# First loads in halves over two queues, a warm-up on constants, unpinned transfers, and a scan whose rounding moves

## The chip, the cores and the metric

The kernel runs on one core of a Trainium2 chip. The metric is the device time of one execution in microseconds (us); the median of three runs of the kernel before is 1250.3 us (1250.12 to 1250.6).

## The reference, cut to what matters

Two independent parts are computed and laid side by side in the last dimension of the output (2048 rows, 1024 + 1024 columns, bf16).

Part A is a diagonal state-space layer: `Bu = x · B_bar^T` with a complex `B_bar`, a scan `h = Lam_bar * h + Bu[t]` over 2048 steps, and `y = 2 Re(h · C^T) + x * D`. Part B is attention over segments of 32 rows with 8 memory rows each, 32 heads of 128:

```python
for s in range(n_seg):
    h = concat([mem, x[:, s*32:(s+1)*32]])       # 8 + 32 rows
    q, k, v = h·Wq, h·Wk, h·Wv
    p = softmax(where(mask, q·k^T * scale, -1e9))
    o = (p·v)·Wo
    mem = o[:, :8];  outs.append(o[:, 8:])
```

## The kernel before, in words

The kernel has four phases; the change touches the first (the pool `p1`, up to about 350 us). That phase computes all values `v = x · Wv` of part B and the first product and scan of part A, woven together. `b.xe` holds part B's x with its 1024 inner elements on the partitions (eight groups of 128) and rows along the free dimension.

**Values.** `Wv` is cut into eight blocks `hb` of 512 columns. For each, sixteen tiles of 128 rows are computed by eight matmuls each (`v_mm`, 128x512, L411) into one of four PSUM banks: `k.ps("A")` alternates between the tags P and S, each with two buffers. ScalarE (ACT) evicts a tile to SBUF (`k.copy("s", ...)`, recorded at L75), and one DMA stores two tiles to a scratch tensor `b_vx` in DRAM (`v_st`, L419). Two tiles make a pair. `v_tile` gives each of the first eight pairs a staging buffer of its own (`st0`), and all later pairs one of two buffers `b_vst`. The generator `values()` takes pairs of blocks 0 and 1 first, then blocks 2 to 7 in order.

**Start.** The first four row tiles of x come as plain rows (`load_rows`, four DMAs of 256 KB) on the queues of SP (SyncE) and ACT, with the weights of block 0 in four quarters. TensorE (PE) turns each by eight transposes with an identity (`turn_rows`), which are then evicted into `b.xe`. Before that, six matmuls on a zeroed tile warm PE up. The rest of x is loaded by transposing DMAs (`load_x` of part B, L367).

**Part A, stage 1.** 32 steps n = 4 pc + tb. Each takes 16 matmuls (L256) of a block of B (`load_b`, two transposing DMAs, L237) with a block of transposed x (`xT[tb]`, `load_x` of part A, one transposing DMA of 1 MB, L231) into one of two `psO` buffers of two banks. VectorE (DVE) multiplies it by cosine and sine tables (L263, L264), subtracts (L266), adds (L267), and runs two scans (L270, L271). The result is rounded to bf16 by ACT and multiplied back by DVE (`post`: L288 to L292). Between steps PE computes three or four value tiles, so that values and scan finish together.

**Order.** The instructions of each engine are placed by a scheduler that follows dependencies and its own estimates. `tc.keep_in_program_order(...)` pins an instruction to its place in the program; an unpinned DMA may be moved past other DMAs of its queue. A DMA signals landing by one of eight semaphores, taken in turn over both queues, so each DMA also waits for the landing of the one eight before it. In the kernel before, the xT loads of part A are pinned, and so are, up to step 3, the value weights of blocks 2 and later and the stores `v_st`.

Of the kernel before, what the change touches and what calls it, by code (L numbers as in the profile page):

```python
# [9 lines left out]
BF16 = mybir.dt.bfloat16  # L10
I32 = mybir.dt.int32
ACT = mybir.ActivationFunctionType
ALU = mybir.AluOpType
# [120 lines left out]
class PartA:  # L134
# [92 lines left out]
    def load_x(self, tb):  # L227
        k = self.k
        self.xT[tb] = k.w8((KC, TB), "xT")
        k.tc.keep_in_program_order(  # L230
            k.SP.dma_start(self.xT[tb], self.x[0][tb * TB:(tb + 1) * TB, :], transpose=True))  # L231

    def load_b(self, pc):
        k = self.k
# [12 lines left out]
    def stage1(self, pc, tb):  # L247
        k = self.k; V, PE = k.V, k.PE
        pin = k.tc.keep_in_program_order
        if tb == 0:  # L250
            self.carry = None
        cs, rot, ed = self.tabs
        u = k.ps("O")
        for i in range(2):
            for c in range(KC):
                m = PE.matmul(u[:, i, :], self.bt[:, i, c, :], self.xT[tb][:, c, :], start=(c == 0), stop=(c == KC - 1))  # L256
                if self.pin:
                    pin(m)
        c_ = cs[:, 0, 0:TB].unsqueeze(1).to_broadcast([128, 2, TB])
        s_ = cs[:, 1, 0:TB].unsqueeze(1).to_broadcast([128, 2, TB])  # L260
        a = self.wp.tile([128, 2, TB], FP32, name="a_a")
        b = self.wp.tile([128, 2, TB], FP32, name="a_b", bufs=1)
        V.tensor_tensor(a[:], u[:], c_, ALU.mult)  # L263
        V.tensor_tensor(b[:], u[:], s_, ALU.mult)  # L264
        wr, wi = a[:, 0, :], a[:, 1, :]
        V.tensor_tensor(wi, wi, b[:, 0, :], ALU.subtract)  # L266
        V.tensor_tensor(wr, wr, b[:, 1, :], ALU.add)  # L267
        rb = self.rr[:, pc:pc + 1].to_broadcast([128, TB])
        ini = self.carry
        pin(V.tensor_tensor_scan(wr, rb, wr, 0.0 if ini is None else ini[:, 0:1], ALU.mult, ALU.add))  # L270
        pin(V.tensor_tensor_scan(wi, rb, wi, 0.0 if ini is None else ini[:, 1:2], ALU.mult, ALU.add))  # L271
        if tb < NB - 1:
            nx = self.wp.tile([128, 2], FP32, name="a_nx"); tt = self.wp.tile([128, 2], FP32, name="a_tt")
            V.tensor_scalar(tt[:], ed[:, 0:2], wi[:, TB - 1:TB], None, ALU.mult)
            V.scalar_tensor_tensor(nx[:], ed[:, 2:4], wr[:, TB - 1:TB], tt[:], ALU.mult, ALU.add)
            self.carry = nx
        if tb not in self.hs:
            self.hs[tb] = self.hsp.tile([128, PC, 2, TB], BF16, name="a_hs", bufs=4)
        self.prev, self.last = self.last, [a, rot, self.hs[tb][:, pc, :, :]]

    def post(self, last):
        if last is None:
            return
        k = self.k; V = k.V
        pin = k.tc.keep_in_program_order
        a, rot, hp = last
        g = self.wp.tile([128, 2, TB], BF16, name="a_g", bufs=1)
        pin(k.S.activation(g[:], a[:], ACT.Copy))  # L288
        n = self.wp.tile([128, 2, TB], BF16, name="a_n", bufs=1)
        pin(V.tensor_tensor(hp, g[:, 0:1, :].to_broadcast([128, 2, TB]), rot[:, 0:2, :], ALU.mult))  # L290
        pin(V.tensor_tensor(n[:], g[:, 1:2, :].to_broadcast([128, 2, TB]), rot[:, 1:3, :], ALU.mult))
        pin(V.tensor_tensor(hp, hp, n[:], ALU.add))  # L292

    def stage2(self, pool, dB):

# [21 lines left out]
class PartB:  # L317
# [48 lines left out]
            if lo < hi:  # L366
                k.SP.dma_start(self.xe[:, :, lo:hi], self.x[0][lo + r:hi + r, :], transpose=True)  # L367

    def load_rows(self, t, n, xr, e):
        e.dma_start(xr[:, t:t + n, :], self.x[0][t * 128 + 64:(t + n) * 128 + 64, :].rearrange("(i p) d -> p i d", p=128))  # L370

    def turn_rows(self, t, xr):

        k = self.k
        pt = k.ps("O", (128, 1024), BF16)
        for c in range(KC):
            k.tc.keep_in_program_order(k.PE.transpose(pt[:, c * 128:(c + 1) * 128], xr[:, t, c * 128:(c + 1) * 128], k.ident[:]))
        k.copy("vs"[t % 2], self.xe[:, :, t * 128:(t + 1) * 128], pt[:].rearrange("p (c n) -> p c n", c=KC))

    def sum_x(self, q, pool):  # L380

# [16 lines left out]
    def load_wv(self, hb, w=None, parts=1, e=None, js=None):  # L398
        if w is None:
            w = self.k.w8((KC, 512), "wv")  # L400
        n = KC // parts
        for i in js or range(parts):
            d = (e or self.k.SP).dma_start(w[:, i * n:(i + 1) * n, :], self.Wf[2][:, i * n:(i + 1) * n, hb * 512:(hb + 1) * 512])
            if self.pin and hb > 1:
                self.k.tc.keep_in_program_order(d)
        return w


# [6 lines left out]
    def v_st(self, hb, q, st, e):  # L415
        vx = self.vx[hb]
        s0 = GX + 2 * q * 128
        n = 2 if q < 7 else 1
        d = e.dma_start(vx[s0:s0 + n * 128, :].rearrange("(i p) n -> p i n", p=128), st[:, 0:n, :])  # L419
        if self.pin:  # L420
            self.k.tc.keep_in_program_order(d)
        if q == 7:
            e.dma_start(vx[0:64, :], st[0:64, 1, :])
            e.dma_start(vx[T - 32:T + 32, :], st[64:128, 1, :])
# [16 lines left out]
    def v_first(self, w, xr, e):  # L441

        k = self.k
        for t in range(3):
            self.turn_rows(t, xr)
        p = [k.ps("A") for t in range(4)]
        for j in range(4):
            for t in range(3):
                self.v_mm(p[t], t, w, range(2 * j, 2 * j + 2))
            if j == 2:  # L450
                self.turn_rows(3, xr)
        self.v_mm(p[3], 3, w, range(KC))
# [393 lines left out]
def kernel_main(tc, A_x, A_Lre, A_Lim, A_Bre, A_Bim, A_Cre, A_Cim, A_logdt, A_Dskip, B_x, B_mem0, B_Wq, B_Wk, B_Wv, B_Wo, out,  # L846
                force=False, dbg=None):
    with ExitStack() as ctx:
        k = K(tc, ctx)
        k.dbg = dbg  # L850
        nc = k.nc
        consts(k)
        a = PartA(k, A_x, A_Lre, A_Lim, A_Bre, A_Bim, A_Cre, A_Cim, A_logdt, A_Dskip, out)
# [11 lines left out]
        with pool("p1", "right") as p1:  # L865
# [6 lines left out]
            a.tab = a.wp = a.btp = b.vst = p1  # L872
            a.jf = b.rall[:, 0:TB + 1]
            xr = tmp[:, 4096:8192].rearrange("p (t d) -> p t d", t=4)
            b.load_rows(0, 1, xr, k.SP)
            b.load_rows(1, 1, xr, nc.scalar)
            b.load_rows(2, 1, xr, k.SP)
            for j in range(4):
                b.load_wv(0, wvs[0], 4, (nc.scalar, k.SP)[j % 2], [j])
            b.load_rows(3, 1, xr, nc.scalar)  # L880
            b.load_wv(1, wvs[1], 2)
            a.load_params(tmp)
            k.SP.dma_start(tmp[0:M, 0:D], b.mem0[0])
            b.load_x(512, 1024)
            b.load_x(1024, 1536)
            b.load_x(1536, T)
            wu = tmp[:, 2048:2560]
            k.V.memset(wu, 0.0)
            pw = k.ps("O")
            for i in range(6):  # L890
                k.PE.matmul(pw[:, i % 2, :], wu[:, 0:128], wu, start=True, stop=True)

            def values():
                yield from b.v_first(wvs[0], xr, k.SP)
# [7 lines left out]
            v = values()  # L902
            done = 0
# [16 lines left out]
            for n in range(PC * NB):  # L920
                pc, tb = n // NB, n % NB
                a.stage1(pc, tb)
                if n in (0, 1):
                    a.load_x(2 + n)
                    wvs[2 + n] = b.load_wv(2 + n)
                if tb == 1 and pc + 1 < PC:
                    nbt = a.load_b(pc + 1)
                want = 20 + 4 * (n + 1) if n < 4 else 36 + (92 * (n - 3) + 27) // 28
                half = done + 2
                while done < want:  # L930
                    next(v, None); done += 1
                    if done == half:
                        a.post(a.prev)
                while done >= 32 and oged < done // 16:
                    b.og(oged, wvs.pop(oged))
                    oged += 1
                if pc + 1 < PC:
                    if tb == 0:
                        tabs = a.tables(pc + 1)
                    else:  # L940
                        next(tabs)
                    if tb == 3:
                        a.tabs, a.bt = a.ntabs, nbt
# [12 lines left out]
            k.V.memset(b.rall[:], 0.0)  # L956
            a.load_c(1, 0)
            a.load_c(1, 1)
# [151 lines left out]
```

## Time and profile before

| What | us |
|---|---|
| median of three runs | 1250.3 |
| profiled execution | 1250.12 |
| its span from first to last instruction | 1248.4 |
| PE busy in the span | 1236.3 |
| DVE busy | 609.4 |
| ACT busy | 329.3 |
| POOL (GpSimd) busy | 199.5 |

The times of the page are from one profiled execution, and start at its first instruction. "SPq" and "ACTq" rows are DMAs as the queue's engine issues them: their time is that of the issue, not of the transfer. In a row of the timeline the first number is the start, the second the duration; a bracket at its end gives the idle time before it and what ended that. In a table of groups, after the bar: busy time, mean ns of one, idle time before them.

### The profile page before, as it was taken

To read this page: it belongs to the slowest core of one execution; us is meant where nothing else is said; L and a number is where in the kernel's file an instruction comes from. 1 tells how busy PE (TensorE), PEld (TensorE's weight loads), DVE (VectorE), ACT (ScalarE), POOL (GpSimd) and SP (SyncE) were. 2 spreads that over 40 slices of the span, in tenths; PEclk is the share of its full clock that TensorE was granted. 3 is DMA by queue.
4 is the path that set the end of the run, shared out by engine and by line. 5 is a ranking of instruction groups with operands and counts; after the bars stand their busy time and mean duration, and the time that the engine had idled before them with its cause. 6 is when DMAs were issued, how large, how long until landed. Compare 5 with 4: busy or idle time off the path is not lost. (4 is left out here: it accounts for less than half of the span.)

```text
span 1248.4 us, 19205 instructions
## 1 busy us (share of the span) xinstructions
PE 1236.3 (99%) x7852; PEld 651.9 (52%) x7923; DVE 609.4 (49%) x1117; ACT 329.3 (26%) x757; POOL 199.5 (16%) x284
## 2 busy tenths in 40 slices
PE   9999999999999999999999999999999999999998
PEld 4444444444455445555555655555556554454443
DVE  4889999999931122444444444444444450011000
ACT  4444434444210002323333333333233320000000
POOL 2000000000032130222222222322232230000000
PEclk9999999999999999999999999999999999999999
DMA  9932232333666557576767544645575469606000
GB/s 238 261 109 68 89 98 71 91 93 85 151 213 201 138 163 139 96 141 141 142 122 156 114 122 94 129 82 94 105 139 105 72 195 217 159 18 152 17 26 19
DMA packets 296995, 151.81 MB, mean 122 GB/s; under 512 B 138440, under 2 KB 290240, under 8 KB 296904
## 3 DMA queue, kind: packets, MB, share of 16 engines
q1 hardware_dynamic: 295640, 149.11, 51.9%
q8 instruction: 63, 1.03, 0.4%
q10 hardware_dynamic: 1264, 1.44, 0.4%
q14 instruction: 28, 0.23, 0.1%
HBM read 73.70 MB, written 43.66 MB: 94 GB/s over the span
## 5 line engine op out<-in xcount | busy, mean ns | idle before, releaser
L570 PE MATMUL psP<-b_xe,w 128*128 128x480 bf16 x2048 | 439.7, 366 | 0.0
L570 PEld LDWEIGHTS <-w 128*128 128x128 bf16 x2048 | 194.2, 98 | 185.2
L603 POOL TENSOR_TENSOR b_m<-b_e,maskB 99x396 bf16<-99x396 bf16 x160 | 139.2, 871 | 356.3 <-ACT b_e L599 356.3
L77 DVE CAST b_q<-psP 128x480 bf16<-128x480 f32 (+1 forms) x192 | 98.2, 533 | 150.9 <-PE psP L570 139.4
L411 PEld LDWEIGHTS <-b_xe 128*128 128x128 bf16 x1024 | 99.9, 98 | 120.4 <-ACT b_xe L75 0.6
L670 PEld LDWEIGHTS <-b_ol 128*128 128x128 bf16 x1024 | 99.5, 98 | 117.5
L75 ACT ACTIVATE b_k<-psP 128x480 bf16<-128x480 f32 x128 | 73.1, 571 | 314.3 <-PE psP L570 314.3
L599 ACT ACTIVATE b_e<-psS 99x396 bf16<-99x396 f32 x176 | 87.4, 496 | 173.8 <-PE psS L596 166.6
L621 DVE TENSOR_TENSOR b_ot<-psO,b_rall 99x512 bf16<-99x512 f32 x176 | 121.7, 692 | 6.4
L256 PE MATMUL psO<-w,a_bt 128*128 128x512 bf16 x496 | 114.8, 379 | 0.8
L670 PE MATMUL psS<-w,b_ol 128*128 128x512 bf16 x438 | 99.0, 379 | 0.6
L619 DVE RECIPROCAL b_rall<-psO 99x4 f32<-99x4 f32 x176 | 31.2, 177 | 136.3 <-PE psO L614 136.2
L411 PE MATMUL psS<-w,b_xe 128*128 128x512 bf16 x378 | 90.1, 379 | 0.4
L411 PE MATMUL psP<-w,b_xe 128*128 128x512 bf16 x376 | 89.8, 379 | 0.4
L256 PEld LDWEIGHTS <-a_bt 128*128 128x128 bf16 x512 | 49.7, 98 | 59.0
L310 PEld LDWEIGHTS <-a_hs 128*128 128x128 bf16 x512 | 49.5, 98 | 58.3
L614 PE MATMUL psO<-b_v,b_m 99*128 99x129 bf16 x704 | 70.5, 221 | 0.1
L77 DVE CAST b_ost<-psS 128x512 bf16<-128x512 f32 x13 | 9.0, 692 | 125.4 <-PE psS L670 112.3
L596 PEld LDWEIGHTS <-b_k 128*128 128x128 bf16 x704 | 49.8, 98 | 33.4 <-issue 0.5
L596 PE MATMUL psS<-b_q,b_k 128*128 128x99 bf16 x704 | 60.1, 208 | 0.2
L75 ACT ACTIVATE b_vst<-psS 128x512 bf16<-128x512 f32 x56 | 33.4, 597 | 98.1 <-PE psS L411 70.2
L310 PE MATMUL psS<-w,a_hs 128*128 128x512 bf16 x245 | 57.3, 380 | 0.6
(201 smaller groups left out, 1084.0 us busy)
## 6 DMA issues: line engine op xcount, KB each, us to landing
b_v<-b_vx SPq DMA_DIRECT2D x16, 1056.0 KB
b_os<-b_ot SPq DMA_DIRECT2D x16, 960.0 KB
w<-in_B_Wv_dram SPq DMA_DIRECT2D x14, 1024.0 KB
b_vx<-b_vst SPq DMA_DIRECT2D x48, 256.0 KB
w<-in_B_Wo_dram SPq DMA_DIRECT2D x12, 1024.0 KB
w<-in_B_Wq_dram SPq DMA_DIRECT2D x16, 512.0 KB
w<-in_B_Wk_dram SPq DMA_DIRECT2D x16, 512.0 KB
a_xn<-in_A_x_dram SPq DMA_DIRECT2D x32, 128.0 KB
```

Of the source, the lines that this page charges most:

```text
L75: self.S.activation(out, in_, ACT.Copy)
L77: self.V.tensor_copy(out, in_)
L256: m = PE.matmul(u[:, i, :], self.bt[:, i, c, :], self.xT[tb][:, c, :], start=(c == 0), stop=(c == KC - 1))
L310: PE.matmul(py[:], self.hs[tb][:, pc, i, tt * 128:(tt + 1) * 128], self.ct[half, i][:, pc, :], start=(pc == 0 and i == 0), stop=(pc == PC ...
L411: m = self.k.PE.matmul(p[:], self.xe[:, c, t * 128:(t + 1) * 128], w[:, c, :], start=(c == 0), stop=(c == KC - 1))
L570: PE.matmul(p[:, 0:480], w[:, i * KC + c, hh * 128:(hh + 1) * 128], self.xe[:, c, 480 * q:480 * q + 480], start=(c == 0), stop=(c == KC - 1))
L596: PE.matmul(s[:, j * GW:(j + 1) * GW], kt[:, hh, g0:g0 + 128], qt[:, hh, g0:g0 + GW], start=True, stop=True)
L599: k.S.activation(e[:], s[0:GW, 0:4 * GW], ACT.Exp, scale=float(E) ** -0.5, accum_out=self.accE[0:GW, i:i + 1])
L603: k.G.tensor_tensor(v4(m[:, 0:4 * GW]), v4(e[:]), mask[0:GW, :, :].unsqueeze(2).to_broadcast([GW, 2, 2, GW]), ALU.mult)
L614: PE.matmul(o[:, gg, cs], m[:, j * GW:j * GW + 128], vt[:, 2 * u + gg, cs], start=True, stop=True)
L621: V.tensor_tensor(ot[:, 2 * u:2 * u + 2, :].rearrange("p g (h e) -> p g h e", h=2), oa[:, :, 1:257].rearrange("p g (h e) -> p g h e", h=2) ...
L670: k.PE.matmul(self.acc[t, half], ol[:, h8, tt * 128:(tt + 1) * 128], self.wo_half(half, h), start=(h == 0), stop=(h == H - 1))
```

## The change

- **Loads at the start.** Each of the four row tiles of x is loaded as two halves of 512 columns, one on SP's queue and one on ACT's, and after each row tile two eighths of block 0's weights follow, one on each queue.
- **Warm-up.** Eight matmuls instead of six, on a constant tile of ones that exists already, instead of a tile that DVE zeroes.
- **Turned tiles.** Value matmuls are placed between the turns as their inputs come; each turn is evicted by two copies on DVE instead of one on DVE or ACT.
- **Pins.** The xT loads of part A, the value weights and the stores of values are no longer pinned.
- **Stage 1.** The subtraction L266 moves to POOL. The rounding on ACT (`round`) is placed behind the next step's matmuls, the multiplication back (`post`) behind the next step's scans, only the first of its three instructions pinned, where before all four were pinned two value tiles into the step after.

```diff
     def load_x(self, tb):
-        k.tc.keep_in_program_order(
-            k.SP.dma_start(self.xT[tb], self.x[0][tb * TB:(tb + 1) * TB, :], transpose=True))
+        k.SP.dma_start(self.xT[tb], self.x[0][tb * TB:(tb + 1) * TB, :], transpose=True)
...
+        self.round()
...
-        V.tensor_tensor(wi, wi, b[:, 0, :], ALU.subtract)
+        k.G.tensor_tensor(wi, wi, b[:, 0, :], ALU.subtract)
...
+        self.post()
         if tb not in self.hs:
             self.hs[tb] = self.hsp.tile([128, PC, 2, TB], BF16, name="a_hs", bufs=4)
-        self.prev, self.last = self.last, [a, rot, self.hs[tb][:, pc, :, :]]
-
-    def post(self, last):
...
-        g = self.wp.tile([128, 2, TB], BF16, name="a_g", bufs=1)
-        pin(k.S.activation(g[:], a[:], ACT.Copy))
-        n = self.wp.tile([128, 2, TB], BF16, name="a_n", bufs=1)
-        pin(V.tensor_tensor(hp, g[:, 0:1, :].to_broadcast([128, 2, TB]), rot[:, 0:2, :], ALU.mult))
-        pin(V.tensor_tensor(n[:], g[:, 1:2, :].to_broadcast([128, 2, TB]), rot[:, 1:3, :], ALU.mult))
-        pin(V.tensor_tensor(hp, hp, n[:], ALU.add))
+        self.last = [a, rot, self.hs[tb][:, pc, :, :]]
+
+    def round(self):
+        if self.last is not None:
+            k = self.k
+            g = self.wp.tile([128, 2, TB], BF16, name="a_g", bufs=1)
+            k.tc.keep_in_program_order(k.S.activation(g[:], self.last[0][:], ACT.Copy))
+            self.last[0] = g
+
+    def post(self):
+        if self.last is None:
+            return
+        V = self.k.V
+        g, rot, hp = self.last
+        self.last = None
+        n = self.wp.tile([128, 2, TB], BF16, name="a_n", bufs=1)
+        self.k.tc.keep_in_program_order(
+            V.tensor_tensor(hp, g[:, 0:1, :].to_broadcast([128, 2, TB]), rot[:, 0:2, :], ALU.mult))
+        V.tensor_tensor(n[:], g[:, 1:2, :].to_broadcast([128, 2, TB]), rot[:, 1:3, :], ALU.mult)
+        V.tensor_tensor(hp, hp, n[:], ALU.add)
...
-    def load_rows(self, t, n, xr, e):
-        e.dma_start(xr[:, t:t + n, :], self.x[0][t * 128 + 64:(t + n) * 128 + 64, :].rearrange("(i p) d -> p i d", p=128))
+    def load_rows(self, t, xr):
+        for i, e in enumerate((k.SP, k.S)):
+            cs = slice(i * 512, (i + 1) * 512)
+            k.tc.keep_in_program_order(e.dma_start(xr[:, t, cs], self.x[0][t * 128 + 64:t * 128 + 192, cs]))
     def turn_rows(self, t, xr):
-        pt = k.ps("O", (128, 1024), BF16)
+        pt = k.ps("O", (128, 2, 1024), BF16)
...
-        k.copy("vs"[t % 2], self.xe[:, :, t * 128:(t + 1) * 128], pt[:].rearrange("p (c n) -> p c n", c=KC))
+        for i in range(2):
+            k.copy("v", self.xe[:, 4 * i:4 * i + 4, t * 128:(t + 1) * 128], pt[:, i, 0:512].rearrange("p (c n) -> p c n", c=4))
...
-            if self.pin and hb > 1:
-                self.k.tc.keep_in_program_order(d)
...
-        if self.pin:
-            self.k.tc.keep_in_program_order(d)
...
     def v_first(self, w, xr, e):
-        for t in range(3):
+        p = [k.ps("A") for t in range(4)]
+        for t, todo in enumerate(((), ((0, 0, 4), (1, 0, 4)), ((0, 4, 6), (1, 4, 6), (2, 0, 6)),
+                                  ((0, 6, 8), (1, 6, 8), (2, 6, 8), (3, 0, 8)))):
             self.turn_rows(t, xr)
-        p = [k.ps("A") for t in range(4)]
-        for j in range(4):
-            for t in range(3):
-                self.v_mm(p[t], t, w, range(2 * j, 2 * j + 2))
-            if j == 2:
-                self.turn_rows(3, xr)
-        self.v_mm(p[3], 3, w, range(KC))
+            for tt, c0, c1 in todo:
+                self.v_mm(p[tt], tt, w, range(c0, c1))
...
-            b.load_rows(0, 1, xr, k.SP)
-            b.load_rows(1, 1, xr, nc.scalar)
-            b.load_rows(2, 1, xr, k.SP)
-            for j in range(4):
-                b.load_wv(0, wvs[0], 4, (nc.scalar, k.SP)[j % 2], [j])
-            b.load_rows(3, 1, xr, nc.scalar)
+            for t in range(4):
+                b.load_rows(t, xr)
+                for j in range(2):
+                    b.load_wv(0, wvs[0], KC, (k.SP, nc.scalar)[j], [2 * t + j])
...
-            wu = tmp[:, 2048:2560]
-            k.V.memset(wu, 0.0)
+            one = nc.const_aps.tensor(1.0, [128, 512], BF16)
...
-            for i in range(6):
-                k.PE.matmul(pw[:, i % 2, :], wu[:, 0:128], wu, start=True, stop=True)
+            for i in range(8):
+                k.PE.matmul(pw[:, i % 2, :], one[:, 0:128], one, start=True, stop=True)
...
-                half = done + 2
                 while done < want:
                     next(v, None); done += 1
-                    if done == half:
-                        a.post(a.prev)
...
-            a.post(a.last)
+            a.round()
+            a.post()
```

More of the change, by code (lines that the diff above doesn't have):

```diff
@@ L276, in stage1 @@
             self.carry = nx
+        self.post()
         if tb not in self.hs:
             self.hs[tb] = self.hsp.tile([128, PC, 2, TB], BF16, name="a_hs", bufs=4)
-        self.prev, self.last = self.last, [a, rot, self.hs[tb][:, pc, :, :]]
-    def post(self, last):
-        if last is None:
-            return
-        k = self.k; V = k.V
-        pin = k.tc.keep_in_program_order
-        a, rot, hp = last
-        g = self.wp.tile([128, 2, TB], BF16, name="a_g", bufs=1)
-        pin(k.S.activation(g[:], a[:], ACT.Copy))
+        self.last = [a, rot, self.hs[tb][:, pc, :, :]]
[7 more added lines that the diff above has]
+        if self.last is None:
+            return
+        V = self.k.V
+        g, rot, hp = self.last
+        self.last = None
         n = self.wp.tile([128, 2, TB], BF16, name="a_n", bufs=1)
-        pin(V.tensor_tensor(hp, g[:, 0:1, :].to_broadcast([128, 2, TB]), rot[:, 0:2, :], ALU.mult))
-        pin(V.tensor_tensor(n[:], g[:, 1:2, :].to_broadcast([128, 2, TB]), rot[:, 1:3, :], ALU.mult))
-        pin(V.tensor_tensor(hp, hp, n[:], ALU.add))
+        self.k.tc.keep_in_program_order(
+            V.tensor_tensor(hp, g[:, 0:1, :].to_broadcast([128, 2, TB]), rot[:, 0:2, :], ALU.mult))
+        V.tensor_tensor(n[:], g[:, 1:2, :].to_broadcast([128, 2, TB]), rot[:, 1:3, :], ALU.mult)
+        V.tensor_tensor(hp, hp, n[:], ALU.add)
     def stage2(self, pool, dB):
@@ L367, in load_x @@
                 k.SP.dma_start(self.xe[:, :, lo:hi], self.x[0][lo + r:hi + r, :], transpose=True)
-    def load_rows(self, t, n, xr, e):
-        e.dma_start(xr[:, t:t + n, :], self.x[0][t * 128 + 64:(t + n) * 128 + 64, :].rearrange("(i p) d -> p i d", p=128))
+    def load_rows(self, t, xr):
+        k = self.k
+        for i, e in enumerate((k.SP, k.S)):
+            cs = slice(i * 512, (i + 1) * 512)
+            k.tc.keep_in_program_order(e.dma_start(xr[:, t, cs], self.x[0][t * 128 + 64:t * 128 + 192, cs]))
     def turn_rows(self, t, xr):
         k = self.k
-        pt = k.ps("O", (128, 1024), BF16)
+        pt = k.ps("O", (128, 2, 1024), BF16)
         for c in range(KC):
-            k.tc.keep_in_program_order(k.PE.transpose(pt[:, c * 128:(c + 1) * 128], xr[:, t, c * 128:(c + 1) * 128], k.ident[:]))
-        k.copy("vs"[t % 2], self.xe[:, :, t * 128:(t + 1) * 128], pt[:].rearrange("p (c n) -> p c n", c=KC))
+            k.tc.keep_in_program_order(k.PE.transpose(pt[:, c // 4, (c % 4) * 128:(c % 4) * 128 + 128], xr[:, t, c * 128:(c + 1) * 128], k.ident[:]))
+        for i in range(2):
+            k.copy("v", self.xe[:, 4 * i:4 * i + 4, t * 128:(t + 1) * 128], pt[:, i, 0:512].rearrange("p (c n) -> p c n", c=4))
     def sum_x(self, q, pool):
@@ L402, in load_wv @@
         for i in js or range(parts):
-            d = (e or self.k.SP).dma_start(w[:, i * n:(i + 1) * n, :], self.Wf[2][:, i * n:(i + 1) * n, hb * 512:(hb + 1) * 512])
-            if self.pin and hb > 1:
-                self.k.tc.keep_in_program_order(d)
+            (e or self.k.SP).dma_start(w[:, i * n:(i + 1) * n, :], self.Wf[2][:, i * n:(i + 1) * n, hb * 512:(hb + 1) * 512])
         return w
@@ L418, in v_st @@
         n = 2 if q < 7 else 1
-        d = e.dma_start(vx[s0:s0 + n * 128, :].rearrange("(i p) n -> p i n", p=128), st[:, 0:n, :])
-        if self.pin:
-            self.k.tc.keep_in_program_order(d)
+        e.dma_start(vx[s0:s0 + n * 128, :].rearrange("(i p) n -> p i n", p=128), st[:, 0:n, :])
         if q == 7:
```

## The prediction

> **What bounds the kernel now.** I read the page's engine shares and clock row first.
>
> ```profile
> PE 1236.3 (99%) x7852; PEld 651.9 (52%) x7923; DVE 609.4 (49%) x1117; ACT 329.3 (26%) x757; POOL 199.5 (16%) x284
> PEclk9999999999999999999999999999999999999999
> ```
>
> TensorE is busy for 1236.3 of 1248.4 us at full clock, so only work or waits on PE can move the end. The table of PE's waits (total, times, longest) is short:
>
> ```profile
> PE psO L891 <- DVE a_hs L888: 1.3, 1, 1.3
> PE psO L377 <- DMA a_hs<-in_B_x_dram: 0.5, 1, 0.5
> PE psO L377 <- DVE b_xe L77: 0.3, 1, 0.3
> ```
>
> All three lie in the first 6.4 us. So the change can gain at most some 2 us at the start, and it can lose wherever it makes PE wait. I therefore looked for the thinnest cover: SyncE's (SP) queue from 25 to 70 us in order of time (start, issue time, engine, line, transfer),
>
> ```profile
> 29.26 4.42 SPq L231 DMA_TRANSPOSE w<-in_A_x_dram  x1
> ...
> 40.27 0.67 SPq L419 DMA_DIRECT2D b_vx<-b_vst  x1
> 40.99 5.59 SPq L231 DMA_TRANSPOSE w<-in_A_x_dram  x1
> 46.67 0.53 SPq L419 DMA_DIRECT2D b_vx<-b_vst  x1
> 47.26 4.78 SPq L231 DMA_TRANSPOSE w<-in_A_x_dram  x1
> 52.09 0.57 SPq L403 DMA_DIRECT2D w<-in_B_Wv_dram  x1
> 52.76 1.07 SPq L419 DMA_DIRECT2D b_vx<-b_vst  x2
> 53.88 7.89 SPq L231 DMA_TRANSPOSE w<-in_A_x_dram  x1
> 61.82 0.57 SPq L403 DMA_DIRECT2D w<-in_B_Wv_dram  x1
> 62.50 7.09 SPq L419 DMA_DIRECT2D b_vx<-b_vst  x3
> ```
>
> then who waits for it on ACT (in brackets: idle time before, and what ended it), and PE beside it,
>
> ```profile
> 59.87 0.60 ACT L75 ACTIVATE b_vst<-psS 128x512 bf16<-128x512 f32 x1 [6.42 <-DMA b_vx<-b_vst]
> ...
> 68.63 0.60 ACT L75 ACTIVATE b_vst<-psS 128x512 bf16<-128x512 f32 x1 [4.82 <-DMA b_vx<-b_vst]
> ```
>
> ```profile
> 56.10 1.89 PE L411 MATMUL psS<-a_hs,b_xe 128*128 128x512 bf16 x8
> ...
> 59.55 1.89 PE L411 MATMUL psS<-a_hs,b_xe 128*128 128x512 bf16 x8
> ```
>
> and the table of stretches (the last columns are granted clock, DMA share, GB/s).
>
> ```profile
> 55.00:60.00 5.00, 5.00 (x25) 2.27 (x24) 3.65 (x4) 0.13 (x1) 0.00 (x0) 1.00 1.10 311
> ```
>
> I number the pairs of value tiles in the order in which they are computed, from 0. Pairs 0 to 7 go to eight buffers of their own; from pair 8 on there are two buffers `b_vst`, so pair 10 may be evicted only when the store of pair 8 has landed, pair 11 after that of pair 9. In the queue above, the stores of pairs 8, 9, 10 and 11, 12 are issued at 40.27, 46.67, 52.76, 62.50. ACT already waits: pair 12's eviction starts at 59.87, 7.1 us after the issue of pair 10's store; pair 14's at 68.63, 6.1 us after that of pair 12's. PE does not, because value tiles have four PSUM banks: pair 12 (56.10) needs pair 10's banks, pair 13 (59.55) those of pair 11. DMA is full there (share 1.10).
>
> **The change, part by part.**
>
> *Start.* Warm-up on constants needs no memset: PE can begin at about 0.9 (DVE's first instruction) instead of 1.33. Its eight matmuls last 8 x 0.43 = 3.4 us, to 4.3; the first turned tile began at 4.54. Halves on two queues bring tile 0 first, where tiles 0 and 1 came together: 0.25 us gained, perhaps 0.2 more as the clock rises earlier (the first 16 turns took 1.5 us, the next 8 took 0.6), and the 0.3 us wait on an eviction, since eight value matmuls now stand before the third tile. Against it: eight completion semaphores are shared in turn, so the loads of tiles 2 and 3 are issued only when the first ones have landed (SP's fifth transfer of before waited for that till 4.68). Bounds: 0.8 us gained to 1 lost; I take 0.4 gained, as the order follows need. Four two-copy evictions on DVE replace two on DVE (0.69) and two on ACT (1.02), under PE's work.
>
> *Order of SP's queue.* Without the pins, the built program issues after the five transposes of x: stores 0, 1, two transposes of B, store 2, xT0, store 3, xT1, store 4, xT2, stores 5, 6, the weights wv2, xT3, stores 7, 8, wv3, store 9, two transposes of B, store 10. So pair 8's store, once issued at 40.27 ahead of xT1, now stands behind all four xT and wv2; pair 9's behind wv3 too. From the rows: stores start at about 25.2 (25.4 before; the start shifts it by some 0.2). With 0.57 a store, 1.33 a B transpose, 4.45 an xT and 0.63 a wv: 25.2 + 1.15 + 2.65 + 0.6 + 4.45 + 0.55 + 4.45 + 0.55 + 4.45 + 1.15 + 0.65 = 45.85. xT3 takes 4.45 at best; in the trace it took 7.89 right behind wv2 and two stores, which is also what stands before it now. I take 7.9: 53.75; stores 7, 8 to 54.9; wv3 to 55.55, when store 9 is issued. Pair 12's store, likewise just behind wv3, released ACT 6.1 us after its issue: 61.7. With the short xT3: 58.2. A second count goes by bytes: the queue is never empty, and when store 9 has landed it has carried what before had carried for store 12, less three stores (256 KB at 311 GB/s, 0.84 each) and two B transposes (256 KB at the 248 GB/s of the stretch 30 to 35 us, 1.06 each): 68.63 - 2.5 - 2.1 = 64.0. Both counts use this queue's own rows; I take 63.0.
>
> *Where it meets PE.* ACT works in order: pair 11's first eviction ends at 63.6, pair 13's first matmul starts at 63.65 instead of 59.55. The wait of pair 12 for pair 8's store (issued about 54.3) is part of these 4.1 us, not added. Queued behind ACT's wait: pair 11's evictions, the rounding of step 0's scan; behind that, DVE's product L299 and its next read of psO, some 9 us late. psO has two buffers, and the one read late is due at 75.2 + 4, so this is covered. xT1, due at 52.65, now comes earlier; later stores have their old places. From there on PE's order is the same, so 4.1 us pass to the end.
>
> *Scan rounding, POOL.* Per step one DVE subtraction goes to POOL, and DVE's second scan waits for it.
>
> ```profile
> L263 DVE TENSOR_TENSOR a_a<-psO,a_cs 128x1024 f32<-128x1024 f32 x32 | 39.0, 1219 | 10.7 <-PE psO L256 10.6
> L215 DVE SCALAR_TENSOR_TENSOR a_rot<-a_cs,a_bre,a_k 128x512 bf16<-128x512 f32 x7 | 5.2, 749 | 6.0 <-ACT a_k L199 6.0
> L305 POOL TENSOR_TENSOR a_xd<-a_xn,a_dB 128x512 f32<-128x512 bf16 x32 | 36.6, 1152 | 71.7 <-DVE a_ot L312 47.6 <-DMA a_xn<-in_A_x_dram 24.0
> ```
>
> Nearest POOL row: 1.15 us. If it runs beside DVE's addition and first scan (0.6 + 1.2 by their starts), DVE saves 0.6 a step; if DVE stands still for all of it, it loses 0.55, over 32 steps 17.6 us, against 16.7 us that it idles. Either way it ends at most some microseconds behind, and psO's buffer is free 12.7 us before its reuse (157.6, 170.3). Cost on PE: 0. If that cover went, each further 0.1 us a step would cost 3.2.
>
> The Trainium skill ("SBUF — State Buffer", Who interferes with whom) speaks against this part: a DVE instruction with two SBUF inputs and a GpSimd one that reads SBUF lock each other out. By it the 0.55 loss holds; no row here shows the two together. The sum stays the same by either.
>
> **Sum.** Profiled execution 1250.1 (span 1248.4 and 1.7 around it); median 0.2 more: 1250.3 + 4.1 = 1254.4.
>
> **Rivals.**
> 1. The queue keeps up. If xT1 to xT3 all issue in 4.45 and store 9 releases ACT by 58.2, pair 13 starts on time, and only the start's gain is left: 1249.9. It decides at a release before 58.5; up to 61.3 the loss stays under 2.5 us. For: xT0 took 4.42 in the same queue. Against: xT1 to xT3 took 4.8 to 7.9, and the byte count. 0.26.
> 2. DVE becomes the bound: POOL's subtraction costs DVE 1 us a step or more, 32 us against 16.7 idle; beyond the 12.7 us of cover PE waits some 3 us more, 1257 with the queue's loss. Against: POOL's row of 1.15. 0.07.
> 3. The start gains over 2.5 us: PE's waits there, 2.1 us, do not hold it. 0.03.
>
> TensorE would idle up to 3 us in one piece. The Trainium skill ("TensorE: Matmul & The Clock Gate", What's actually happening) halves the clock after about 3.4 idle us; no row here shows a pause of that length once PE is warm. By that page an estimated 1.7 us would come on top; the sum leaves it out.
>
> **Numbers.** The forecast, with a loss of 2.5 to 6 us: 0.64. About 0.2%, 2.5 us, can be told from no change. Slower: 0.64 + 0.07 = 0.71; same 0.26; faster 0.03. Range: from rival 1, 1249.7, to the byte count's 64.0 (+5.1) with a late xT and rival 2, 1257.2.
>
> **What would show it.** Right: ACT's evictions of pairs 10 and 11 released by `b_vx<-b_vst` near 58 and 63; PE L411 waiting on ACT near 56 and 62, 3 to 5 us in all; nothing on PE after 70. Wrong: no such wait, or PE L256 waiting on DVE after 100 us.

## The result and the profile after

The changed kernel takes 1259.6 us (median of four runs, 1259.18 to 1262.32) against 1250.4 us before on the same chip: the ratio is 1.0078, with a 95% interval of 1.0061 to 1.0096. It is slower, as forecast, but by 9.2 us instead of 4.1, and the time lies above the stated range, which ended at 1257.2. The profiled execution took 1259.18 us, its span 1257.5.

First the page of after, engine shares and clock:

```profile
PE 1238.6 (98%) x7854; PEld 652.3 (52%) x7925; DVE 621.4 (49%) x1090; ACT 325.8 (26%) x755; POOL 253.7 (20%) x316
PEclk9999999999999999999999999999999999999999
```

TensorE's work has hardly changed (+2.3 us busy), so the loss must stand in its waits. The table of PE's waits in after (total, times, longest; two more waits at the start, of 0.9 and 0.4 us, follow below these rows):

```profile
PE psS L421 <- ACT b_vst L75: 5.4, 1, 5.4
PE psS L318 <- ACT b_vst L75: 1.3, 1, 1.3
PE psO L388 <- DMA a_hs<-in_B_x_dram: 0.9, 1, 0.9
```

Two waits on ACT are new. The first is the forecast one; the second, at the end of stage 1, was not forecast. PE's timeline in after shows the first in its place:

```profile
53.10 3.62 PE L255 MATMUL psO<-w,a_bt 128*128 128x512 bf16 x16
62.14 3.54 PE L421 MATMUL psS<-a_hs,b_xe 128*128 128x512 bf16 x8 [5.43 <-ACT b_vst L75]
65.51 1.89 PE L421 MATMUL psP<-a_hs,b_xe 128*128 128x512 bf16 x8
67.24 1.89 PE L421 MATMUL psS<-a_hs,b_xe 128*128 128x512 bf16 x8
```

Pair 12 waits 5.43 us, and its first eight matmuls then take 3.54 us instead of 1.89. Pair 13 starts at 67.24 instead of 59.55, 7.7 us late. The table of stretches gives the reason for the slow eight (last columns: granted clock, DMA share, GB/s):

```profile
50.00:75.00 25.00, 19.47 (x82) 8.38 (x82) 12.00 (x13) 5.29 (x9) 3.72 (x2) 0.93 0.88 235
```

A granted clock of 0.93 over 25 us is one of 0.5 over some 3.5 us. The page's clock row, in slices of 31 us, does not show it. Now SP's queue and ACT in after, to be laid beside the lists of before:

```profile
28.07 1.02 SPq L429 DMA_DIRECT2D b_vx<-a_hs  x2
...
43.27 4.96 SPq L230 DMA_TRANSPOSE w<-in_A_x_dram  x1
48.33 1.04 SPq L429 DMA_DIRECT2D b_vx<-a_hs  x2
49.42 0.49 SPq L415 DMA_DIRECT2D w<-in_B_Wv_dram  x1
49.96 7.64 SPq L230 DMA_TRANSPOSE w<-in_A_x_dram  x1
57.69 0.53 SPq L429 DMA_DIRECT2D b_vx<-a_hs  x1
58.32 0.41 SPq L429 DMA_DIRECT2D b_vx<-b_vst  x1
58.78 0.49 SPq L415 DMA_DIRECT2D w<-in_B_Wv_dram  x1
59.36 0.70 SPq L429 DMA_DIRECT2D b_vx<-b_vst  x1
```

```profile
61.49 0.60 ACT L75 ACTIVATE b_vst<-psS 128x512 bf16<-128x512 f32 x1 [17.96 <-DMA b_vx<-b_vst]
...
66.06 0.60 ACT L75 ACTIVATE b_vst<-psS 128x512 bf16<-128x512 f32 x1 [3.48 <-DMA b_vx<-b_vst]
```

The order is the one forecast: four xT and the weights of block 2 ahead of the first `b_vst` store, those of block 3 ahead of the second. The times are not. The stores begin at 28.07, not 25.2; pair 8's store is issued at 58.32 and frees ACT at 61.49, 3.2 us later; pair 9's at 59.36, behind 1 MB of weights, frees ACT at 66.06, 6.7 us later.

For the second wait, DVE and POOL by groups in after (busy time, mean ns of one, idle before):

```profile
L266 POOL TENSOR_TENSOR a_a<-a_a,a_b 128x512 f32<-128x512 f32 x32 | 54.1, 1689 | 294.7 <-DVE a_b L264 271.1 <-ACT b_vst L75 23.5
L270 DVE TENSOR_TENSOR_SCAN a_a<-a_rr,a_nx,a_a 128x512 f32<-128x512 f32 x24 | 45.8, 1910 | 0.6
L263 DVE TENSOR_TENSOR a_a<-psO,a_cs 128x1024 f32<-128x1024 f32 x32 | 38.9, 1215 | 0.2 <-PE psO L255 0.2
```

The scan that runs beside POOL's subtraction takes 1910 ns; in before the same group took 1283. DVE stood idle for 10.7 us ahead of L263 in before, nearly all of it waiting for PE, and for 0.2 now: it is behind almost all the way, and at the end of stage 1 PE waits 1.26 us for ACT, which waits for DVE:

```profile
355.85 3.61 PE L318 MATMUL psS<-w,a_hs 128*128 128x512 bf16 x15 [1.26 <-ACT b_vst L75]
```

### The profile page after: what moved, and what is told of

It reads as the page before. It is cut to its first block, busy times and chain, and to the rows that moved or that the text cites. A ratio compares the mean times of both kernels' runs of the same rounds, so it can differ in the third digit from the quotient of the medians.

```text
span 1257.5 us, 19279 instructions
## 1 busy us (share of the span) xinstructions
PE 1238.6 (98%) x7854; PEld 652.3 (52%) x7925; DVE 621.4 (49%) x1090; ACT 325.8 (26%) x755; POOL 253.7 (20%) x316
## 5 line engine op out<-in xcount | busy, mean ns | idle before, releaser
L255 PE MATMUL psO<-w,a_bt 128*128 128x512 bf16 x498 | 114.8, 379 | 0.7
L266 POOL TENSOR_TENSOR a_a<-a_a,a_b 128x512 f32<-128x512 f32 x32 | 54.1, 1689 | 294.7 <-DVE a_b L264 271.1
L318 PEld LDWEIGHTS <-a_hs 128*128 128x128 bf16 x512 | 49.5, 98 | 59.7 <-issue 1.4
L255 PEld LDWEIGHTS <-a_bt 128*128 128x128 bf16 x512 | 49.7, 98 | 59.0
L287 ACT ACTIVATE a_g<-a_a 128x1024 bf16<-128x1024 f32 x32 | 33.8, 1056 | 113.4 <-DVE a_hs L298 111.1
```

Source lines behind the costliest of these rows:

```text
L266: k.G.tensor_tensor(wi, wi, b[:, 0, :], ALU.subtract)
```

## The experiments

The runs form four groups, each on a chip of its own with the kernel before beside it: e1 to e4, e5 to e8, e9 to e12, e13 to e16. Before took 1250.2 to 1250.9 us there. Times inside the kernel come from one profiled execution of each run. "Behind stage 1" is the start of the first product after the first phase in the profiled execution (L310 in before, L318 in after): 346.74 in before, 355.85 in after.

| Run | edit | median us | ratio to before, interval | behind stage 1 |
|---|---|---|---|---|
| e1 | after, pins back | 1251.82 | 1.0009, 1.0 to 1.0018 | 347.43 |
| e2 | after, L266 on DVE | 1257.79 | 1.0053, 1.004 to 1.0067 | 355.57 |
| e3 | after, both | 1250.99 | 1.0001, 0.9992 to 1.001 | 347.05 |
| e5 | before, pins removed | 1261.1 | 1.0085, 1.0071 to 1.0099 | 356.05 |
| e6 | before, L266 on POOL | 1250.55 | 1.0001, 0.9992 to 1.001 | 346.41 |
| e7 | before, new start | 1250.73 | 1.0004, 0.9995 to 1.0014 | 346.76 |
| e8 | before, new warm-up | 1250.39 | 0.9999, 0.999 to 1.0008 | 346.99 |
| e11 | after, one xT pinned | 1254.78 | 1.0039, 1.0026 to 1.0053 | 350.19 |
| e12 | e5, block 3's weights later | 1259.49 | 1.0073, 1.006 to 1.0087 | 355.17 |
| e4 | after, 25 filler matmuls | 1259.07 | 1.0062, 1.0048 to 1.0076 | 355.48 |
| e9 | after again | 1258.91 | 1.0069, 1.0056 to 1.0083 | 357.11 |
| e13 | after again | 1259.25 | 1.007, 1.0057 to 1.0084 | 355.44 |
| e10 | after, 16 filler matmuls | 1258.92 | 1.0073, 1.0059 to 1.0087 | 355.39 |
| e14 | after, 16 in step 1's buffer | 1258.33 | 1.0065, 1.0052 to 1.0079 | 354.75 |
| e15 | after, pair 9's store early | 1266.43 | 1.0123, 1.0107 to 1.0138 | 356.21 |
| e16 | e14 and e15 | 1264.54 | 1.0113, 1.0097 to 1.0128 | 352.89 |

### Which part of the change costs what

e1 puts the pins back into after, e2 the subtraction, e3 both:

```diff
-        k.SP.dma_start(self.xT[tb], ..., transpose=True)
+        k.tc.keep_in_program_order(
+            k.SP.dma_start(self.xT[tb], ..., transpose=True))
...
+            if self.pin and hb > 1:
+                self.k.tc.keep_in_program_order(d)
...
+        if self.pin:
+            self.k.tc.keep_in_program_order(d)
```

```diff
-        k.G.tensor_tensor(wi, wi, b[:, 0, :], ALU.subtract)
+        V.tensor_tensor(wi, wi, b[:, 0, :], ALU.subtract)
```

> After with the pins of the xT loads, the value weights and the stores put back, all else as changed. Theory Q (the order of SP's queue makes the stall, and the stall makes the half clock): pair 12's wait of 5.43 and the 1.64 behind it go together, 7.1 us; the start's 0.45 and the 1.3 at the end of stage 1 stay: 1259.2 - 7.1 = 1252.1. Rival M (the rounding that now stands behind the next step's matmuls holds ACT, and so pair 12's banks): a stall of 3 us or more stays near 57, 1255 to 1259. Rival S (the later start of the queue alone is enough): stores still land late, PE waits 2 to 3 us near 57, 1254 to 1255.

> After with the subtraction L266 on DVE again. Theory Q with P (GpSimd's subtraction locks DVE's scan out, so DVE falls behind and ACT's rounding with it): the wait of 1.3 at the end of stage 1 goes, the first scan L270 is back from 1.91 to 1.28 us, the stall of 5.4 near 57 stays: 1259.2 - 1.3 = 1257.9. Rival M' (the moved rounding itself makes the wait at the end, whichever engine subtracts): the 1.3 stays, 1259.2.

> After with the pins put back and the subtraction on DVE: what is left is the start and the moved rounding. Theory: only the start's 0.45 us stays, 1250.1 + 0.45 = 1250.6 to 1250.9; no wait of PE over 0.5 us after 20 us. Rival M or M': 1252 or more, with a wait of PE on ACT. Rival G (the start is a gain that the later waits hide): under 1250.0.

The pins alone bring the time back to 0.9 us above before, so some 8 of the 9 us are the order of SP's queue; the place of the rounding makes no stall near 57 us (rival M falls). The table of PE's waits in e1 keeps the wait at the end of stage 1:

```profile
PE psS L319 <- ACT b_vst L75: 1.0, 1, 1.0
```

It is gone in e2 and e3, where DVE subtracts. e2's 1257.8 is what the theory gave, but its interval (1.004 to 1.0067) overlaps that of after (1.0056 to 1.0083 in e9), so that the missing wait shows the effect, and the median alone does not. With both edits nothing measurable is left.

e5 goes the other way, before with only the pins removed; e6, e7 and e8 add one other part each to before: the subtraction on POOL; the loads in halves, the weave and the warm-up; the warm-up alone.

> Before with only the three pins removed; first loads, warm-up, subtraction and rounding as before. Theory Q: the queue's new order alone makes a stall near 57. Its SP queue starts its stores at 25.4 instead of 28.1, 2.7 us earlier than in after, and store 8 stands behind the same transfers: the stall is 5.43 - 2.7 = 2.7 us, too short to lower the clock if theory C holds: 1250.1 + 2.7 = 1252.8. This is also what the prediction's sum (4.1) should have been measured on: 1254.2 by it. Rival S (the queue's late start alone makes it): 1250.1.

> Before with only the subtraction L266 on POOL, all pins and the old place of the rounding kept. Theory P: the first scan takes about 1.9 us instead of 1.28, DVE's lag grows over the steps, and PE waits at the end of stage 1 by up to 1.3 us: 1250.1 to 1251.5. With the old place of the rounding, two value tiles later, less may reach PE, so 1250.3 is as likely as 1251.4. Rival L (the lock costs 1 us a step and DVE becomes the bound): 1253 or more.

> Before with only the first loads in halves, the weave and the warm-up on ones. Theory: pair 3's first matmul comes 0.45 us later than before, since the eight semaphores hold tiles 2 and 3 back; the queue's pinned order has room for its later start: 1250.1 + 0.45 = 1250.6. Rival G: faster, 1249.7 (the prediction's term). Rival S (late stores without any change of order make PE wait): over 1252.

> Before with only the warm-up: eight matmuls on the constant ones, no memset. PE starts at about 0.9 instead of 1.33, and its eight matmuls end by 4.3, before the first turned tile can begin (4.54 before). The first turns run at a higher clock, where sixteen took 1.5 us and the next eight 0.6: 0.2 to 0.4 us gained if nothing else holds the start, 1249.8; rival: the value weights and the evictions set the start, no change, 1250.2.

e5 contradicts its expectation, 1252.8: it is at least as slow as after, though its queue starts its stores at 25.3. The queue and ACT in e5 show why:

```profile
48.30 6.99 SPq L230 DMA_TRANSPOSE w<-in_A_x_dram  x1
55.38 0.53 SPq L416 DMA_DIRECT2D b_vx<-a_hs  x1
55.97 0.46 SPq L402 DMA_DIRECT2D w<-in_B_Wv_dram  x1
56.52 0.83 SPq L416 DMA_DIRECT2D b_vx<-b_vst  x1
```

```profile
62.92 0.60 ACT L75 ACTIVATE b_vst<-psS 128x512 bf16<-128x512 f32 x1 [19.79 <-DMA b_vx<-b_vst]
```

The scheduler, free to order, has put the weights of block 3 ahead of pair 8's store here. That store is issued 1.8 us earlier than in after and lands 1.4 us later. So the late start of the queue is not needed for the loss, and e7 shows that it is not enough either: there the stores start at 27.67 in the pinned order, and the time is that of before:

```profile
27.67 1.02 SPq L423 DMA_DIRECT2D b_vx<-a_hs  x2
```

e6 costs nothing measurable, nor does the moved rounding in e3; the two together cost 0.8 us (e1 against e3) and 1.0 to 1.3 us of wait. How late DVE starts the first product of the last three steps shows it: 0.04 us in each in before; 0.27, 0.46, 0.65 in e6; 0.33, 0.79, 1.24 in e3; 5.77, 6.51, 7.24 in e1. With one part alone DVE catches up again and again (0.04 us behind at step 22 in e6, 0.23 in e3, steps counted from 0); with both it stays more than 2 us behind from step 11 on, and the last steps add 0.7 us each. DVE has no room in the last steps: in before it runs without an idle row from 323.56 to 340.83, two steps of 8.63 us. What each part adds there can be read from the rows: 0.2 us a step in e6, and 0.45 in e3, where DVE now stands idle ahead of its second multiplication (L299 in after) until ACT has rounded, as in after:

```profile
345.97 0.69 DVE L299 TENSOR_TENSOR a_n<-a_g,a_rot 128x1024 bf16<-128x1024 bf16 x1 [0.46 <-ACT a_g L287]
...
355.34 0.69 DVE L299 TENSOR_TENSOR a_n<-a_g,a_rot 128x1024 bf16<-128x1024 bf16 x1 [0.45 <-ACT a_g L287]
```

No run has the subtraction on POOL and the moved rounding without the new start, so a share of the start in this is not excluded.

### What makes a store land late

e11 pins only the xT load of step 3; e12 is e5 with block 3's weights requested at step 3.

```diff
-        k.SP.dma_start(self.xT[tb], ..., transpose=True)
+        d = k.SP.dma_start(self.xT[tb], ..., transpose=True)
+        if tb == 3:
+            k.tc.keep_in_program_order(d)
```

```diff
-                    wvs[2 + n] = b.load_wv(2 + n)
+                if n in (0, 3):
+                    wvs[2 + n // 3] = b.load_wv(2 + n // 3)
```

> After with only the fourth xT load (step 3's) pinned: in the queue it now stands behind the stores of pairs 8 to 11, but two 256 KB transposes of B go ahead of pair 8's store. Byte theory (a store lands when the queue has moved all bytes ahead of it; 1 MB less 0.5 MB at 250 to 311 GB/s): pair 8's store lands 1.7 to 2.1 us earlier than in after, near 59.5; PE waits 3.3 to 3.7 us, half clock just at its edge: 1256.0 to 1257.9. Issue theory (what counts is the time that SP's instructions take; 7.6 less 2.7 us): it lands 4.9 us earlier, near 56.5, PE waits under 1 us: 1252.5 to 1253.5.

> Before without the pins, as in the earlier run that came out slower than after (7.3 us of wait, pair 8's store issued at 56.52 and its buffer free at 62.92), but with the weights of block 3 loaded at step 3 instead of step 1: in the queue one 256 KB transpose of B stands ahead of pair 8's store where 1 MB of weights stood. Byte theory: 0.79 MB less ahead, at 250 to 311 GB/s 2.5 to 3.2 us: the buffer is free near 60, PE waits 4.1 to 4.8 us instead of 7.3, 1257.5 to 1258.6 against 1261.1. Issue theory: a weight load costs SP 0.5 us and a transpose of B 1.3 to 2.5, so the store is issued later than before, 57.3 or more, and the wait is no shorter: 1261 or more.

SP's queue in e11 and then in e12, and below them the row of ACT that pair 8's store releases in each:

```profile
51.82 2.49 SPq L238 DMA_TRANSPOSE a_bt<-in_A_B_im_dram  x1
54.41 5.54 SPq L431 DMA_DIRECT2D b_vx<-b_vst  x4
```

```profile
57.19 0.53 SPq L416 DMA_DIRECT2D b_vx<-b_vst  x1
57.78 1.28 SPq L236 DMA_TRANSPOSE a_bt<-in_A_B_im_dram  x1
59.11 0.57 SPq L402 DMA_DIRECT2D w<-in_B_Wv_dram  x1
59.78 1.92 SPq L416 DMA_DIRECT2D b_vx<-b_vst  x2
```

```profile
57.49 0.60 ACT L75 ACTIVATE b_vst<-psS 128x512 bf16<-128x512 f32 x1 [13.95 <-DMA b_vx<-b_vst]
```

```profile
60.23 0.60 ACT L75 ACTIVATE b_vst<-psS 128x512 bf16<-128x512 f32 x1 [16.88 <-DMA b_vx<-b_vst]
```

Neither theory holds for both. In e11 the store frees its buffer 4.0 us earlier than in after, nearer to the issue theory (4.9) than to the byte theory (2.1), PE waits 1.4 us, and the time lies between the two forecasts. In e12 it is issued 0.7 us later than in e5 and frees its buffer 2.7 us earlier, as the byte theory has it; the time misses that theory's range all the same (1259.5 against 1257.5 to 1258.6), since pair 9's store, now right behind the weights, holds PE for another 1.81 us ahead of pair 13. One account fits the stores of these runs: the issue of a transposing DMA of 1 MB takes SP 4.1 to 8.3 us, and so delays the issue of the store behind it; a plain load of 1 MB takes SP 0.5 us, but the store right behind it takes longer to land. From issue to release it is 3.1 us in e11, 3.0 in e12 and 3.2 in after where no weights stand just ahead, and 6.4 (e5), 6.7 (pair 9 in after) and 7.6 us (pair 9 in e12) where they do; with one transpose between (pair 9 in e5) it is 4.5. Why the store lands later behind a plain load is not shown; the 3.3 to 4.5 us more are near the 3.4 to 4.2 us that 1 MB would take, by an estimate from the 250 to 311 GB/s of the forecasts.

### How much is the half clock

e4 fills the place where PE stood still in after with 25 matmuls on the constant ones, e10 with 16; e9 is after itself.

```diff
                 a.stage1(pc, tb)
+                if n == 1:
+                    fil = k.ps("O")
+                    for i in range(25):
+                        tc.keep_in_program_order(k.PE.matmul(fil[:, i % 2, :], one[:, 0:128], one, start=True, stop=True))
```

> After with 25 matmuls on the constant ones (128x512, 0.216 us each, 5.4 us) put behind step 1's product, where PE stood still; they write a psO buffer that nobody reads. Theory C (PE's idle 5.43 in one piece halves the granted clock for the eight matmuls behind it): pair 12 starts at about 62.1 as before but takes 1.9 us instead of 3.54, 1259.2 - 1.6 = 1257.6. Rival D (the slow eight matmuls come from the full DMA queues or from memory at that time, not from the pause): 1259.2, eight matmuls of 427 ns again. If the queue had room and the filler merely delayed PE: over 1260.

> The changed kernel itself, so that the runs beside it are compared on one chip: 1259.6 again, pair 12 waiting about 5.4 us near 57 and its eight matmuls at 427 ns.

> After with 16 constant matmuls (3.5 us) instead of 25 in the place where PE stands still. They leave some 2 us of the pause, so that pair 12 is not delayed even where the start of the run was 1.5 us later. Theory C (the length of the pause lowers the clock): pair 12 starts with its store as in after, near 62, all its matmuls take 216 ns, and the run is 1.6 us or more below after of the same call, near 1257.7; mean clock 0.999 instead of 0.996. Rival D (the clock falls by what the DMA queues do, or by the restart itself): as after, 1259.6.

In both the slow matmuls are gone (pair 12 takes 1.73 us a tile, the mean clock is 0.999 instead of e9's 0.996), and in both the time is that of after. So the pause did cause the half clock, but my price for it, 1.6 us, falls. Only e10 judges the price: in e4 step 1 began 1.7 us later than in after, and the filler held pair 12 until 63.71. PE's timeline in e10 shows what is late next:

```profile
61.49 1.89 PE L421 MATMUL psS<-a_hs,b_xe 128*128 128x512 bf16 x8
63.22 1.89 PE L421 MATMUL psP<-a_hs,b_xe 128*128 128x512 bf16 x8
65.80 1.89 PE L421 MATMUL psS<-a_hs,b_xe 128*128 128x512 bf16 x8 [0.69 <-ACT b_vst L75]
67.53 1.89 PE L421 MATMUL psP<-a_hs,b_xe 128*128 128x512 bf16 x8
70.23 3.63 PE L255 MATMUL psO<-w,a_bt 128*128 128x512 bf16 x16 [0.81 <-DVE a_b L264]
```

Pair 13 now waits for pair 9's store, and step 2's product for a psO buffer, of which the filler had taken one. e14 therefore writes the 16 matmuls into step 1's own buffer ahead of its product; e15 pins the weights of block 3 and the second block of B behind the stores of pairs 9 to 13; e16 does both, and e13 is after again.

```diff
         u = k.ps("O")
+        if pc == 0 and tb == 1:
+            one = k.nc.const_aps.tensor(1.0, [128, 512], BF16)
+            for i in range(16):
+                pin(PE.matmul(u[:, i % 2, :], one[:, 0:128], one, start=True, stop=True))
```

```diff
+            d = k.SP.dma_start(bt[:, i, :, :], w[pc * 128:(pc + 1) * 128, :], transpose=True)
+            if pc == 1:
+                k.tc.keep_in_program_order(d)
...
+            if hb == 3:
+                self.k.tc.keep_in_program_order(d)
...
+                if n in (0, 3):
+                    wvs[2 + n // 3] = b.load_wv(2 + n // 3)
+                if tb == (1, 2)[pc == 0] and pc + 1 < PC:
```

> The changed kernel again, for comparison on one chip: 1258.9 to 1259.6. Pair 9's store should land near 66.0, and pair 13 start between 66.7 (if the clock is back by then) and 68.5 (if it comes back late).

> After with 16 constant matmuls ahead of step 1's product, written into that product's own psO buffer, which the product then overwrites: no buffer is taken from step 2, and the pause ahead of pair 12 shrinks from 5.4 to about 2 us. Theory T (two limits side by side: pair 8's store and the half clock behind its pause, and pair 9's store, which lands near 66.0): all of pair 12's matmuls at 216 ns, pair 13 waits for pair 9's store and starts at 66.7; 0.5 to 1.8 us below after of the same call, by how long the clock stayed down there. Theory C alone (the half clock lies on the path in full, 1.6 to 3 us): 2 us or more below after. Rival D (the clock falls without a pause of over 3 us too): as after.

> After with the weights of block 3 and the second block of B pinned behind the stores of pairs 9 to 13 in the queue, so that pair 9's store follows pair 8's at once and lands near 62 instead of 66. Theory T: pair 12 still waits 5.4 us for pair 8's store and runs at half clock, so pair 13 starts at 67.2 to 68.5, as in after: within 0.5 us of after of the same call. Theory N (pair 9's store alone sets the loss): pair 13 starts some 3 us earlier, 1256 to 1257.

> Both edits, the late loads and the 16 constant matmuls. Theory T: with pair 9's store early and no half clock, pair 12 starts near 62.1 and pair 13 at 65.6, step 2's product at 69.1 instead of 70.7 to 72.0: 1.6 to 2.9 us below after of the same call, more than the two edits give alone added up. Theory C alone: no more than with the constant matmuls alone. Theory N: no more than with the late loads alone.

In e15 and e16 PE also waits between 587 and 597 us, in the attention of part B, where after does not; their medians are therefore no measure, and I compare the start of step 2's product, and the row behind stage 1. PE's timeline at pair 13 and step 2 in e14, then in e15, then in e16:

```profile
66.03 1.89 PE L425 MATMUL psS<-a_hs,b_xe 128*128 128x512 bf16 x8 [0.45 <-ACT b_vst L75]
...
69.48 3.62 PE L259 MATMUL psO<-w,a_bt 128*128 128x512 bf16 x16
```

```profile
61.27 3.57 PE L425 MATMUL psS<-a_hs,b_xe 128*128 128x512 bf16 x8 [4.47 <-ACT b_vst L75]
64.64 3.15 PE L425 MATMUL psP<-a_hs,b_xe 128*128 128x512 bf16 x8
...
71.08 3.62 PE L257 MATMUL psO<-w,a_bt 128*128 128x512 bf16 x16
```

```profile
60.97 1.89 PE L429 MATMUL psS<-a_hs,b_xe 128*128 128x512 bf16 x8 [1.07 <-ACT b_vst L75]
...
67.87 3.62 PE L261 MATMUL psO<-w,a_bt 128*128 128x512 bf16 x16
```

Step 2's product starts at 70.30 in e13, after on the same chip (70.69 and 71.98 in the other profiles of after), at 69.48 without the half clock, at 71.08 with pair 9's store early (the clock came back late there, as the second row shows), and at 67.87 with both: one edit alone gains 0.8 us or nothing, both together 2.4. This is what theory T forecast (1.6 to 2.9 for both, more than the two alone): the half clock and pair 9's store are two limits that lie side by side, and taking away one leaves the other. The evidence is one profiled execution of each, but e16 starts 2.4 us ahead of the earliest of after's three. The half clock itself lies on the path for 0.6 us in the profiled execution of after (pair 13 could start at 66.66, when ACT had evicted, and started at 67.24), for 1.1 us in that of e13 (65.78 and 66.84) and for 1.9 us in that of e9 (66.58 and 68.53). By the medians e14 is 0.9 us below e13, but the two intervals overlap almost wholly, so the medians alone do not show it.

## Why the prediction was right or wrong

**The mechanism was right.** The unpinned xT loads and weights go ahead of the stores, pairs 10 and 11 cannot be evicted in time, and PE stands still ahead of pair 12 (5.43 us; ahead of pair 13 it has no wait of its own, since pair 12 at half clock lasted longer). Putting the pins back removes it (e1), and taking the pins alone out of before brings it about (e5).

**The step that failed is the issue time of the stores on SP's queue.** It was worked out as 55.55 for pair 9 and measured as 59.36. Of these 3.8 us, 2.9 are there when the first store is issued (28.07 against 25.2): the five transposes of x start at 10.96 instead of 9.04, behind four more loads on this queue and the later landings that they wait for, and take 16.99 us instead of 16.25. The prediction moved the queue's start by only 0.2. Another 1.1 are the first three xT (14.4 us against 3 x 4.45); the rest of the queue took 0.2 less than the sum. But e5 and e7 forbid us to call the start the cause of the loss: an early start without the pins lost as much, a late start with the pins lost nothing. What share of the 9 us it has in after itself no run separates.

**From issue to release** 6.1 us were taken and 6.7 measured. Pair 9's release came at 66.06 where 63.0 was taken; of the two counts the one by bytes (64.0) was the nearer, the one by issue (61.7) the farther, and e11 and e12 show that neither is right alone. That is 3.1 of the 5.0 us by which the sum fell short of the profile's 9.1.

**The clock** was left out of the sum because no row of before had such a pause. The Trainium skill ("TensorE: Matmul & The Clock Gate", What's actually happening) has the clock halved after an idle window of about 3.4 us, and by it the prediction named an estimated 1.7 us on top. The half clock came, over 3.4 us in this profile, but on the path it was 0.6: the rule gives the slow stretch, and not what else is late beside it. Of the three profiles of after this is the mildest (1.1 in e13, 1.9 in e9).

**POOL and the rounding** were taken at zero, and cost 1.3 at the end of stage 1 in this profile, where the prediction expected nothing on PE after 70 us. By the groups, a step lost 0.63 us on the first scan and 0.24 on L267 and saved 0.69 on L266, some 0.2 net; the prediction's 0.55 of loss was a bound that holds. What failed is the cover: 16.7 us of DVE's idle time and 12.7 at one psO buffer were set against the whole, but the last steps have no room at all, and the moved rounding, which was given no price, adds 0.45 us to each there, more than POOL's 0.2. The place was missed too: PE waited not at L255 but behind the last step. The rows agree with the lock between the engines that the prediction cites (the Trainium skill, "SBUF — State Buffer", Who interferes with whom): 1.91 to 2.12 us for a scan of 1.28, while POOL's operation takes 1.69 to 1.77.

**The start** was forecast as a gain of 0.4 us. No run shows one: e7 differs from before by 0.3 us, e8 by 0.1, both within their intervals. In after pair 3 starts at 18.15 instead of 17.70, but at 17.86 in e9, 17.43 in e13 and 17.72 in e7, so that no fixed loss is shown either. It is no part of the sum, since pair 13 then waits for a store whatever PE did before.

No run came out below before by more than can be told; e6 and e8 are level with it.

In sum, by the profiled execution: pair 9's release 7.1 us on pair 13, the half clock 0.6, the end of stage 1 1.3, together 9.0 of 9.1.

## What to carry to other kernels

A pin on a DMA queue can be worth more than the work it orders: where a buffer is freed by a store, look at what the scheduler may put ahead of that store, and count a transposing load as time of the issuing engine and a plain load as time until the next store lands. When a wait is removed or filled and the time stays, look for the next limit at the same place, and test the two together. Cover must be read in the steps where it is thinnest, and two edits that are each covered may share that cover.

## What the runs showed of the hardware

- The granted clock fell to half after pauses of PE of 4.35 to 7.25 us (after, e2, e5, e9, e12, e13, e15) and not after 1.07, 1.42 and 1.81 us (e16, e11, and pair 13 in e12). Read in windows of 0.1 us, it stayed there for 3.41 us (after, e12) or for 6.83 us, twice as long (e2, e5, e9, e13, e15), and it fell 2.7 (e13) to 5.4 us (after) after PE had stopped; in after and e12 that was as PE started again or 0.7 us behind it. This fits a window that runs freely against the program, as the section on the clock gate has it (3.4 us).
- The length of the pause alone does not decide: at the start of e14 PE paused for 2.19 us only, and the clock was at half from 6.92 to 10.34 us. So the window need not be idle as a whole, where the section speaks of an idle window; the measurement decides.
- The start varies likewise: after eight warm-up matmuls from 0.85 us on, the matmuls ran at full speed from 4.2 us in after, and from about 10 us in e4 and e10, so that step 1's product began at 54.78 and 54.54 instead of 53.10; the later wait hid it. This is read from their spacing (427 or 216 ns), as the column of the granted clock reads 1.00 there from the start.
- A 256 KB transposing load of B took 1.28 to 1.30 us of SP's queue with no weights just ahead (after at 29 us, e12 at 57.78), and 2.3 to 3.1 behind a load of weights (after near 60, e5, e11); one took 2.5 behind six stores (e16 at 69.11).
